# Attention and MoE on one core: softmax weights of the first four pairs turned on TensorE instead of VectorE, products with v over 128 keys, order refitted

## The chip, the cores and the metric

One NeuronCore of a Trainium2 chip runs the whole program in one launch. The metric is the device time of that launch in microseconds; lower is better. Engines are named as in the profile: PE (matmul), PEld (its weight loads), DVE, ACT, POOL, and SP, which issues the DMAs.

## The reference

Inputs are q, k, v of 4 batches x 8 heads x 576 positions x 64, and two MoE matrices, 512 x 2048 and 2048 x 512, all float32.

```python
q_rot, k_rot = rotate(q), rotate(k)              # rotary embedding over the 64 head dims
scores = q_rot @ k_rot.T / sqrt(64)
attn = exp(scores - max(scores));  attn = attn / (sum(attn) + 1e-9)
x = concat_heads(attn @ v)                       # 2304 tokens x 512
h = x @ w_in                                     # 2304 x 2048
g = h * sigmoid(1.702 * h)
out = g @ w_out                                  # 2304 x 512
```

## The kernel before

The 32 heads are worked in 16 pairs; four pairs make one batch. For a pair, `prep_qk` (L413) loads q and k, rotates them on POOL or DVE (rope, L441 to L445), turns them on PE (L450) and copies them to KP (L349 on ACT, L351 on DVE). `scores` (L480) makes a pair's nine tiles of 128 queries x 576 keys (eight of one head each, the ninth with the last 64 queries of both) on PE (L492) into SPS, a PSUM buffer of two banks. `softened` (L500) takes each tile through three steps: DVE negates it into the SBUF tile TP and keeps the minimum (L505), ACT takes the exponential and its sum in place (L508), DVE turns it in place, block by block of 32 x 32 (L511). `weighted` (L535) then multiplies by v over 32 keys at a time: v is loaded to 32 partitions (L470) and copied from there to the other three groups of 32 (L476, the tile VR), and each of 18 key blocks takes eight small matmuls, four row groups by two column halves (L559). The results go to XS (`bring`, L569). `inverse_sums` (L514) brings the reciprocal sums through DRAM to all partitions (r_dram), and `attention` (L589) multiplies, splits the result into a rounded part and its remainder, and stores both to x_dram (L604).

Beside that, 32 weight blocks are loaded, repaired in their bits and split into two float32r parts (`weight`, L612), the first sixteen of them ahead of the MoE. `moe` (L659) works on 256 tokens: it loads both parts of x (XC, L665) and, for each of 16 blocks of 128 hidden units, does twelve matmuls (L681), tanh on ACT (L687), DVE and POOL steps, and six matmuls with w_out (L698). The last four token blocks go through `two_chunks` (L746), which saves products by sums and differences (L822, L863). The first token block needs all four pairs of the first batch.

No order is written out by hand. A planner (`Plan`, L74) knows each step's durations and buffers, and places on each engine, among the steps that are ready, the one with the lowest priority number; the table of numbers at L19 to L38 sets these. Every engine then runs its list strictly in that order. Buffers have few slots: SPS three, PT (one PSUM bank each) two, TP and XS two for the first four pairs (L40, L41) and one later. `n_wide` = 4 marks the first four pairs: only for them may all slots of SPS and PT be taken, since the MoE does not run yet.

Of the kernel before, what the change touches and what calls it, by code (L numbers as in the profile page):

```python
# [10 lines left out]
F32 = mybir.dt.float32  # L11
F32R = mybir.dt.float32r
# [6 lines left out]
PLANNED = dict(wait=300.0, wait_dve=300.0, wait_pool=300.0, n_split=2, n_early=4, n_warm=12, n_wide=4, n_pv0=4,  # L19
               n_pv=2, rope=67526.1, turn=28154.573, raw=-70793.084, v_at=35677.739, exp=95827.369, across=-2250.108,  # L20
               pv_at=88.518, pv_step0=-3821.97, pv_step=41180.485, out_at=-37554.001, prep_s1=48754.242,
               prep_s2=50905.361, sums=-2.997, x_at=0.024, w_raw=12434.947, tanh=-73344.369, g_hi=-83328.381,
               mm2=13528.64, x_load=-38305.217, sums_at=-58928.512, shared_at=-58312.958, t_load=41561.566)
PREP_AT = [-431652, -283537, -243401, 152515, -30818, 30946, 226554, 310380, 369343, 400429, 415121, 453550, 556628,
           575478, 633426, 708309]
PAIR_AT = [-193357, -46411, 4523, 116548, 19858, -52329, -18421, 357094, 447016, 101083, 572080, -23019, 84854,
           402937, 548884, 761647]
PAIR_LEN = [70053, 59678, 65344, -45458, 29105, 157197, 13871, -7478, -59624, -167984, 31814, 209302, 102692, 16421,
            10423, 16592]
MOE_AT = [76876, 312003, 14034, -137881, 278470, 398587, 756302, -263235, 109992, 344381, 521867]  # L30
MOE_STEP = [-765, -55664, -95070, 45956, -63589, 17457, 21326, 60007, 15778, -45369, -18925]
WEIGHT_AT = [-287246, -91871, -93899, -9546, 127995, -371991, -66861, 623510, -246095, 46024, -89938, -116240, 184586,
             513457, -13419, 329611, -149145, 169832, -968684, 64148, 311802, 196893, 295771, 136903, 179235, -30254,
             106295, 327664, 338864, 49395, 458477, 614589]
WEIGHT_FROM = [-100755, 45903, 44044, 8010, 38392, 72497, 110866, 45430, -16026, -66328, -27523, 52698, -161139,
               -28138, -71686, -137246, 51453, 98771, -24675, 29431, 84389, 66452, -49724, 101137, -31460, -18730,
               -83530, 2900, -63136, 114168, -16225, 45606]
T_AT = [292094, -401508, 518576, 614296, 354139, 589559, 140258, 949997]  # L38
MORE_TIMES = ['T_AT']
SLOTS = dict(SPS=3, PT=2, RAW=2, RAW1=1, BT=1, KP=2, ST=2, RT=3, XS=1, XC=4, T=1, G=1, O=2, OW=2, CW=2, TP=1, VR=1)  # L40
EARLY = dict(RAW=2, RAW1=1, BT=1, XS=1, KP=1, TP=1, VR=1, OW=3, CW=3)  # L41
# [32 lines left out]
class Plan:  # L74
# [24 lines left out]
    def op(self, durs, fn, deps=(), bufs=(), prio=0.0, moved=None, chain=None, columns=0.0,  # L99
           release=0.0, port=(), mode=("", ""), code=0.0):  # L100
        o = Op(len(self.ops), durs, fn, list(bufs), prio, moved, columns, release, port, mode, code)
        for d in {id(d): d for d in deps if d is not None}.values():
            d.out.append(o)
            o.before += 1
        if chain is not None:
            if chain in self.chains:
                self.chains[chain].then.append(o)
                o.before += 1
            self.chains[chain] = o
        for b in o.bufs:  # L110
            b.users.append(o)
        self.ops.append(o)
        return o
# [172 lines left out]
def attention_moe(ctx: ExitStack, tc: tile.TileContext, q, k, v, w_in, w_out, cos_sin, out):  # L286
# [17 lines left out]
                 XS=([128, 2, S], F32), XC=([128, KD, CT], F32R), TP=([128, 9, S], F32), VR=([128, 2, S // 32, D], F32),  # L304
# [101 lines left out]
    constants = op(POOL, 1200.0, f, prio=-1e6)  # L406

# [53 lines left out]
    def prep(n):  # L461
        p0 = PREP_AT[n]
        is_early = n < at["n_early"]
        kq_of[n], st_of[n], vr = buf("KP", is_early), buf("ST", is_early), buf("VR", is_early)
        kq_ready[n] = [prep_qk(n, s, p0 + (0.0, at["prep_s1"], at["prep_s2"])[s]) for s in range(3)]
        b, j = divmod(n, PPB)

        def f():
# [31 lines left out]
    def softened(n, t, s, mm, prio):  # L500
# [9 lines left out]
            bufs=[st, tp], prio=prio + at["exp"], extra=228)  # L510
        return o, vec("DVE", "psum", S, lambda e: nc.vector.transpose(tp.t[:, t], tp.t[:, t]), o, bufs=[tp],  # L511
# [23 lines left out]
    def weighted(n, turned, xs, prio):  # L535
# [5 lines left out]
        if n < at["n_wide"]:  # L541
            held = plan.buf("SPS"), plan.buf("PT"), plan.buf("PT")
            banks = lambda: (held[0].t[:, 0], held[0].t[:, 1], held[1].t, held[2].t)
        else:
            held = plan.buf("SPS", (0, 1)), plan.buf("SPS", (0, 1))
            banks = lambda: tuple(x.t[:, i] for x in held for i in range(2))
        n_key, o = S // 32, None
        n_part, step = (at["n_pv0"], at["pv_step0"]) if n < at["n_wide"] else (at["n_pv"], at["pv_step"])
        runs = lambda h, i: (0, 4 + (i < 2)) if not h else (4 + (i < 2), 9)
        for part in range(n_part):  # L550
            keys = range(n_key * part // n_part, n_key * (part + 1) // n_part)

            def f(keys=keys):
                for a in keys:
# [7 lines left out]
            o = pe(f, turned, vr_ready[n], o, f32=[160] * len(keys), each_code=11 if n < at["n_early"] else 8, extra=90.0,  # L562
                   mode=("small", "small"),
# [3 lines left out]
        last = lambda i: slice(512 + 32 * (i % 2), 544 + 32 * (i % 2))  # L567
# [4 lines left out]
        for m in range(2):  # L572
            r, c0, c1 = slice(64 * m, 64 * m + 64), 32 * m, 128 * (1 - m)
            src = held[m]
            if n < at["n_wide"] and m:
                for i in range(2):
                    x = held[1 + i]
                    bring(x, 128, lambda x=x: x.t[:, c0:c0 + 128].rearrange("p (t q) -> p t q", t=4), lambda i=i: tiles()[:, 2 + i])
                    bring(x, 32, lambda x=x: x.t[r, c1:c1 + 32], lambda i=i: xs.t[r, 1, last(i)])
                continue  # L580
# [4 lines left out]
        return done  # L585

    x_written = {}

    def attention(n):  # L589
# [4 lines left out]
        done = weighted(n, [x[2] for x in got], xs, p0 + at["pv_at"] * u)  # L594
# [377 lines left out]
```

## Time and profile before

| | |
|---|---|
| median of 3 runs | 696.7 us (696.59 to 701.07) |
| the profiled execution's own time | 697.98 us |
| its span, first to last instruction | 696.3 us |
| mean granted PE clock | 0.962 |
| busy: PE / DVE / ACT / POOL | 645.9 / 488.3 / 350.3 / 265.5 us |

The profile is of one execution. Busy times are the union of an engine's instructions, so that overlapping ones count once; the means of a group count each in full. A matmul in float32 leaves two records of matmul and two of weight loads in the trace. The granted clock is the share of full speed that PE was given, 0.5 or 1.0 at any moment (1.2 or 2.4 GHz).

### The profile page before, as it was taken

The page shows a single profiled execution, that of the slowest core. Times are in us where ns is not written, and L with a number is a line of the kernel's source. Part 1 is how long each engine was busy: PE and PEld are TensorE (multiplying, and loading weights), DVE is VectorE, ACT ScalarE, POOL GpSimd, SP SyncE. Part 2 cuts the span into 40 slices and gives each one's busy share as a digit, 9 for nine tenths or more (in the row PEclk, how much of TensorE's full clock was granted, in tenths as well). Part 3 has the DMA queues.
Part 4 walks back from the last instruction along what each step waited for, and adds up shares of the span by engine and source line. Part 5 has one row for each costly group of instructions (what it writes and reads, how often), then busy time and mean ns, then how long its engine had stood idle before and what let it go on. Part 6 is the DMA issues. An engine that isn't in the chain of part 4 may idle for free.

```text
span 696.3 us, 19494 instructions
## 1 busy us (share of the span) xinstructions
PE 645.9 (93%) x7928; PEld 524.7 (75%) x7928; DVE 488.3 (70%) x1070; ACT 350.3 (50%) x863; POOL 265.5 (38%) x269
## 2 busy tenths in 40 slices
PE   6588776899999999999999999999999999999996
PEld 4356553777778777788887878787878899988985
DVE  4998998698899888968966583847369544644342
ACT  2776766375576554545445352544234444543343
POOL 3776675364745354667644531220102100120000
PEclk8888987799999999999999999999999999999999
DMA  7866786956866655394556450543076223342111
GB/s 150 212 191 162 185 207 199 242 155 155 256 173 187 149 168 157 127 339 144 150 188 163 119 120 20 124 123 79 11 274 213 74 109 122 121 169 75 61 62 60
DMA packets 98506, 104.35 MB, mean 150 GB/s; under 512 B 62560, under 2 KB 82288, under 8 KB 93808
## 3 DMA queue, kind: packets, MB, share of 16 engines
q1 hardware_dynamic: 98416, 103.10, 51.7%
q8 instruction: 62, 1.02, 0.6%
q14 instruction: 28, 0.23, 0.1%
HBM read 65.26 MB, written 23.67 MB: 128 GB/s over the span
## 4 chain that ended last, share of the span: by engine, by line
PE 73%; DVE 8%; DMA 5%; issue 4%; POOL 3%; SPq 3%; ACT 3%; DVEq 0%; POOLq 0%; ACTq 0%
PE PT L681 15%; PE SPS L698 13%; PE SPS L863 13%; PE SPS L559 10%; PE SPS L492 9%; PE SPS L822 6%; PE PT L822 5%; DVE TP L505 2%; DVE TP L511 2%; PE PT L450 2%; DMA t_dram<-TS 1%; SPq L531 1%; DMA OW<-in_moe_w_out_dram 1%; DMA XS<-r_dram 1%; POOL RAW L354 1%
## 5 line engine op out<-in xcount | busy, mean ns | idle before, releaser
L681 PEld LDWEIGHTS PT<-XC,win 128*128 128x128 f32 x960 | 125.7, 193 | 21.2 <-issue 10.9
L681 PE MATMUL PT<-XC,win 128*128 128x256 f32 x960 | 136.3, 291 | 3.6 <-issue 2.6
L698 PE MATMUL SPS<-wout,G 128*128 128x512 f32 x480 | 132.6, 406 | 2.8 <-DVE G L354 1.4
L508 ACT ACTIVATE TP<-TP,ST 128x576 f32<-128x576 f32 x144 | 110.8, 771 | 46.3 <-DVE TP L505 46.0
L492 PE MATMUL SPS<-KP 64*128 64x288 f32 (+1 forms) x640 | 111.2, 457 | 10.9 <-DVE TP L505 9.1
L511 DVE STREAM_TRANSPOSE TP<-TP 128x576 f32<-128x576 f32 x144 | 108.3, 768 | 15.9 <-ACT TP L508 15.7
L505 DVE TENSOR_SCALAR_CACHE_REDUCE TP<-SPS 128x576 f32<-128x576 f32 x144 | 103.5, 747 | 10.6 <-PE SPS L492 10.0
L698 PEld LDWEIGHTS SPS<-wout,G 128*128 128x128 f32 x480 | 83.7, 189 | 29.8 <-issue 8.7
L559 PE MATMUL SPS<-TP,VR 32*64 32x128 f32 (+1 forms) x4032 | 96.3, 304 | 4.5 <-issue 2.9
L559 PEld LDWEIGHTS SPS<-TP,VR 32*64 32x64 f32 x4032 | 84.3, 136 | 15.6 <-issue 10.2
L863 PE MATMUL SPS<-wout,G 128*128 128x512 f32 x384 | 93.0, 392 | 0.0
L492 PEld LDWEIGHTS SPS<-KP 64*128 64x128 f32 (+1 forms) x640 | 58.1, 188 | 45.2 <-DVE TP L505 17.7
L354 DVE TENSOR_TENSOR G<-T,G 128x256 fp32r<-128x256 f32 x122 | 57.4, 483 | 43.1 <-ACT G L342 32.6
L863 PEld LDWEIGHTS SPS<-wout,G 128*128 128x128 f32 x384 | 70.4, 188 | 13.9
L342 ACT CAST G<-T 128x256 fp32r<-128x256 f32 x115 | 44.9, 404 | 57.2 <-PE SPS L698 38.3
L648 POOL TENSOR_TENSOR CW<-CW 128x512 int32<-128x512 int32 x32 | 41.4, 1300 | 58.4 <-DVE RAW L354 17.9
L354 POOL TENSOR_TENSOR XS<-XS 128x576 fp32r<-128x576 f32 (+1 forms) x25 | 35.6, 1423 | 61.0 <-DVE XS L344 39.5
L687 ACT ACTIVATE T<-PT 128x256 f32<-128x256 f32 x80 | 30.4, 380 | 53.5 <-PE PT L681 39.6
L689 DVE SCALAR_TENSOR_TENSOR T<-T,PT 128x256 f32<-128x256 f32 x80 | 32.7, 409 | 33.3 <-ACT T L687 33.1
L354 POOL TENSOR_TENSOR U<-U,U 128x256 f32<-128x256 f32 x15 | 11.6, 772 | 113.3 <-ACT U L342 111.4
L354 POOL TENSOR_TENSOR BT<-RAW,cos_sin_sb 128x512 f32<-128x512 f32 (+1 forms) x30 | 31.9, 1063 | 29.5 <-DMA RAW<-in_k_dram 9.8
L450 PE MATMUL PT<-ident,RAW 128*128 128x128 f32 x144 | 26.3, 298 | 17.4 <-issue 6.8
(94 smaller groups left out, 853.9 us busy)
## 6 DMA issues: line engine op xcount, KB each, us to landing
TR<-t_dram SPq DMA_DIRECT2D x16, 1024.0 KB, 4.8
VR<-VR SPq DMA_DIRECT2D x48, 288.0 KB, 4.0
x_dram<-XS SPq DMA_DIRECT2D x16, 576.0 KB, 4.6
XC<-x_dram SPq DMA_DIRECT2D x18, 512.0 KB, 5.3
OW<-in_moe_w_in_dram SPq DMA_DIRECT2D x16, 512.0 KB, 5.0
OW<-in_moe_w_out_dram SPq DMA_DIRECT2D x16, 512.0 KB, 5.2
t_dram<-TS SPq DMA_DIRECT2D x8, 1024.0 KB, 5.9
VR<-in_v_dram SPq DMA_DIRECT2D x32, 144.0 KB, 3.5
```

What stands on the lines that cost most here:

```text
L342: return nc.scalar.copy(to, src)
L354: return engine[e].tensor_tensor(to, a, b, op=how)
L492: nc.tensor.matmul(ss[h].t[:, c, 0:HALF] if t < 4 else ss[h].t[rows, c, 0:HALF], kq.t[rows, 1, t * 128:t * 128 + (128 if t < 4 else 64)], ...
L505: o = vec("DVE", "psum", S, lambda e: nc.vector.tensor_scalar(tp.t[:, t].rearrange("p (c s) -> p c s", c=2), s.t[:, :, 0:HALF], -1.0, LARG ...
L508: o = vec("ACT", "sbuf", S, lambda e: nc.scalar.activation(tp.t[:, t], tp.t[:, t], AF.Exp, bias=st.t[:, 0, t:t + 1], scale=-1.0, accum_out ...
L511: return o, vec("DVE", "psum", S, lambda e: nc.vector.transpose(tp.t[:, t], tp.t[:, t]), o, bufs=[tp], prio=prio + at["exp"] + at["across"])
L559: nc.tensor.matmul(bank[64 * h:64 * h + 64, to:to + 32 * (s1 - s0)], vr.t[rows, h, a], tp.t[rows, s0:s1, 32 * a:32 * a + 32], start=(a == ...
L648: o = vec("POOL", "two", DM, lambda e, a=a, r=r: nc.gpsimd.tensor_tensor(a().bitcast(I32), a().bitcast(I32), r(), op=ALU.add), o, low, buf ...
L681: nc.tensor.matmul(h.t[:, 0:CT], win[f_i // KH][:, wl, kk, f_i % KH * 128:(f_i % KH + 1) * 128], xc[xl].t[:, kk, :], start=(i == m == 0), ...
L698: nc.tensor.matmul(acc.t[:, m, :], g.t[:, a, m * 128:(m + 1) * 128], wout[f_i // KH][:, b, f_i % KH, :], start=(f_i == fs[0] and i == 0), ...
L822: nc.tensor.matmul(h(to), w(a)[:, k], x(b)[:, k], start=(begin and n == 0), stop=(n == 5), skip_group_check=True)
L863: nc.tensor.matmul(acc[j].t[:, m, :], g.t[:, x, m * 128:(m + 1) * 128], wout[f_i // KH][:, y, f_i % KH, :], start=(begin and n == 0), stop ...
```

## The change

For the first four pairs the DVE turn of L511 is gone. In the new `weighted_whole` PE turns each tile's first 512 keys in four 128 x 128 blocks into PT, and ACT or DVE copies them back to the same place of TP; the last 64 keys of eight tiles are turned in pairs, and the ninth tile's by two more. v is loaded once with keys on 128 partitions (the tile VE, two slots; the last 64 keys of both heads share one block, with zeros beside them from POOL), and the products run over 128 keys, one column half of the array for each head. They use one SPS buffer and no PT. KP gets one slot more for the first pairs, and all numbers of the planner's table are new, with a list of single adjustments (NUDGE) beside them.

```diff
-PLANNED = dict(wait=300.0, wait_dve=300.0, wait_pool=300.0, n_split=2, n_early=4, n_warm=12, n_wide=4, n_pv0=4,
+PLANNED = dict(wait=300.0, wait_dve=300.0, wait_pool=300.0, n_split=2, n_early=4, n_warm=12, n_wide=4, n_pv=2,
...
+NUDGE = {240: -4973, 292: -1266, 328: 1607, 399: -5780, 422: -10019, 423: 6925, 1070: 1165, 1071: 9102, 1139: 3669,
...
-EARLY = dict(RAW=2, RAW1=1, BT=1, XS=1, KP=1, TP=1, VR=1, OW=3, CW=3)
+EARLY = dict(RAW=2, RAW1=1, BT=1, XS=1, KP=2, TP=1, VE=2, OW=3, CW=3)
...
+        prio = prio + NUDGE.get(len(self.ops), 0.0)
...
+        for x in plan.tiles["VE"]:
+            nc.gpsimd.memset(x[0:64, 4, 1], 0.0)
+            nc.gpsimd.memset(x[64:128, 4, 0], 0.0)
...
+            for h in range(2):
+                nc.sync.dma_start(vr.t[:, 0:4, h], v[b, 2 * j + h, 0:512].rearrange("(t p) d -> p t d", p=128))
+                nc.sync.dma_start(vr.t[64 * h:64 * h + 64, 4, h], v[b, 2 * j + h, 512:576])
...
+        if n < at["n_wide"]:
+            return o, o
         return o, vec("DVE", "psum", S, lambda e: nc.vector.transpose(tp.t[:, t], tp.t[:, t]), o, bufs=[tp],
...
-        if n < at["n_wide"]:
-            held = plan.buf("SPS"), plan.buf("PT"), plan.buf("PT")
-            banks = lambda: (held[0].t[:, 0], held[0].t[:, 1], held[1].t, held[2].t)
...
+    def weighted_whole(n, ready, xs, prio, turn_at):
...
+        def turn(cols, get, ready, moves, pr):
+            pt = plan.buf("PT")
+
+            def f():
+                for i in range(cols // 128):
+                    src = get(i)
+                    for h, x in enumerate(src):
+                        r = both(h) if len(src) > 1 else slice(0, 128)
+                        nc.tensor.matmul(pt.t[r, 128 * i:128 * i + 128], x, ident, start=(i == 0), stop=(i == cols // 128 - 1),
+                                         is_transpose=len(src) == 1, skip_group_check=True)
...
+            for width, to, src in moves:
+                turned.append(vec("ACT DVE", "psum", width, lambda e, to=to, src=src: copy(e, to(), src(pt.t)), o,
+                                  bufs=[tp, pt], prio=pr + at["across"]))
...
+        for t, o in ready.items():
+            turn(512, lambda i, t=t: [tp.t[:, t, 128 * i:128 * i + 128]], o,
+                 [(512, lambda t=t: tp.t[:, t, 0:512], lambda x: x)], turn_at[t])
...
+        av, o = plan.buf("SPS"), None
+        for part in range(2):
+            def f(part=part):
+                for kt in (0, 1) if part == 0 else (2, 3):
+                    for h in range(2):
+                        nc.tensor.matmul(av.t[both(h), 0, :], ve.t[:, kt, h], tp.t[:, 5 * h:5 * h + 4, 128 * kt:128 * kt + 128],
+                                         start=(kt == 0), stop=False, skip_group_check=True)
...
+        return [vec("ACT DVE", "psum", w, lambda e, c=c, w=w: copy(e, xs.t[:, 1, 512 * c:512 * c + w], av.t[:, c, 0:w]), o,
+                    bufs=[av, xs], prio=pr) for c, w in ((0, 512), (1, 64))]
```

Line numbers of the new kernel are higher: the eviction L505 is L527, the exponential L508 is L530, ACT's and DVE's copies L342 and L344 are L346 and L348, the scores L492 are L514, the sums' turn L524 is L548, the turn of q and k L450 is L462. New are the turn L615 and the products L639 (512 columns), L643, L649 and L652.

On DVE, in the first pair (TP_101), evictions and turns stood in turn before the change:

```order
L505 TENSOR_SCALAR TP_101,ST_95<-SPS_65 128x576
L505 TENSOR_SCALAR TP_101,ST_95<-SPS_67 128x576
L351 TENSOR_SCALAR KP_94<-PT_68 128x512
L511 STREAM_TRANSPOSE TP_101<-TP_101 128x576
L505 TENSOR_SCALAR TP_101,ST_95<-SPS_65 128x576
L505 TENSOR_SCALAR TP_101,ST_95<-SPS_66 128x576
L511 STREAM_TRANSPOSE TP_101<-TP_101 128x576
```

And now, at the same tiles:

```order
L527 TENSOR_SCALAR TP_101,ST_95<-SPS_65 128x576
L527 TENSOR_SCALAR TP_101,ST_95<-SPS_66 128x576
L348 COPY TP_101<-PT_68 128x512
L527 TENSOR_SCALAR TP_101,ST_95<-SPS_65 128x576
L527 TENSOR_SCALAR TP_101,ST_95<-SPS_67 128x576
L527 TENSOR_SCALAR TP_101,ST_95<-SPS_66 128x576
L348 COPY TP_101<-PT_68 128x512
```

The turns are gone from DVE; of the 36 wide copies back eight stand on it, and 28 on ACT.

On PE, between the second pair's scores (KP_94) and the first pair's products, the order before was:

```order
L492 MATMUL SPS_65<-KP_94 128x288
L492 MATMUL SPS_66<-KP_94 128x288
L450 MATMUL PT_68<-ident,RAW_107 128x128 x4
L524 MATMUL PT_69<-ident,ST_95 9x128
L559 MATMUL SPS_67<-TP_101,VR_102 64x160 x2
L559 MATMUL PT_68<-TP_101,VR_102 64x128
L559 MATMUL PT_69<-TP_101,VR_102 64x128
```

And now:

```order
L514 MATMUL SPS_65<-KP_94 128x288
L514 MATMUL SPS_67<-KP_94 128x288
L615 MATMUL PT_68<-ident,TP_113 128x128 x4
L548 MATMUL PT_69<-ident,ST_95 9x128
L639 MATMUL SPS_66<-TP_101,VE_114 64x512 x2
L643 MATMUL SPS_66<-TP_101,VE_114 64x64 x2
L639 MATMUL SPS_66<-TP_101,VE_114 64x512 x2
L643 MATMUL SPS_66<-TP_101,VE_114 64x64 x2
L615 MATMUL PT_68<-ident,TP_113 128x128 x4
L615 MATMUL PT_69<-ident,TP_113 128x128 x4
```

Where 144 small matmuls of a pair stood there are 20 large ones, and between them, and between the score groups, stand turns of the next pair's tiles, which take both PT slots.

On SP, at the first loads of XC, the order before was (the store of the fourth pair's result to x_dram stands six rows ahead of this piece):

```order
L431 DMA RAW_91<-in_k_dram 64x64
L665 DMA XC_70<-x_dram 128x4x256
L665 DMA XC_71<-x_dram 128x4x256
L526 DMA r_dram<-RT_97 9x128
L665 DMA XC_72<-x_dram 128x4x256
```

And now (XS_110 holds the fourth pair's result):

```order
L681 DMA x_dram<-XS_110 128x2x576
L439 DMA RAW_90<-in_q_dram 128x4x64 x2
L709 DMA OW_117<-in_moe_w_in_dram 128x4x256
L550 DMA r_dram<-RT_97 9x128
L742 DMA XC_70<-x_dram 128x4x256
L742 DMA XC_71<-x_dram 128x4x256
```

The fifth pair's reciprocal sums (r_dram) now go out ahead of the first XC loads and not behind two of them. Before the first MoE matmul PE has the same sets of work in both kernels, the scores and products of five pairs, and one score group of the sixth more in the new one.

## Rows read from the trace of the kernel before

**Rows 1.** The page: busy time, and busy tenths and granted clock in 40 slices
```profile
PE 645.9 (93%) x7928; PEld 524.7 (75%) x7928; DVE 488.3 (70%) x1070; ACT 350.3 (50%) x863; POOL 265.5 (38%) x269
...
PE   6588776899999999999999999999999999999996
...
DVE  4998998698899888968966583847369544644342
...
PEclk8888987799999999999999999999999999999999
```

**Rows 2.** Busy us by stage: length, engines (instructions), granted clock, DMA share, GB/s
```profile
0.00:128.30 128.30, 94.25 (x1733) 66.06 (x1733) 110.84 (x242) 77.35 (x185) 74.56 (x74) 0.84 0.74 188
128.30:139.00 10.70, 8.05 (x39) 6.35 (x40) 5.11 (x11) 4.93 (x12) 4.63 (x5) 0.68 1.00 254
139.00:348.00 209.00, 202.91 (x2772) 161.47 (x2770) 181.09 (x378) 120.88 (x284) 118.72 (x114) 0.99 0.64 180
348.00:696.30 348.30, 340.67 (x3394) 290.87 (x3390) 191.28 (x441) 147.13 (x382) 67.56 (x79) 1.00 0.36 114
```

**Rows 3.** Chain of waits, end of the first stage: start us, us, what
```profile
117.07 1.35 DVE TP L511 x2
...
120.67 4.40 PE SPS L559 x119
...
125.66 2.65 PE SPS L559 x111
128.31 0.55 PE PT L681 x3
128.87 2.65 issue
131.51 2.29 PE PT L681 x9
```

**Rows 4.** Groups by line, shapes apart, 0 to 128.3 us: busy us, mean ns, idle before
```profile
L511 DVE STREAM_TRANSPOSE TP<-TP 128x576 f32<-128x576 f32 x45 | 33.6, 766 | 4.1 <-ACT TP L508 4.0
L505 DVE TENSOR_SCALAR_CACHE_REDUCE TP<-SPS 128x576 f32<-128x576 f32 x45 | 32.2, 745 | 3.4 <-PE SPS L492 3.3
L349 ACT ACTIVATE KP<-PT 128x512 f32<-128x512 f32 x11 | 6.5, 596 | 16.4 <-PE PT L450 16.3
L351 DVE TENSOR_SCALAR KP<-PT 128x512 f32<-128x512 f32 x3 | 2.0, 674 | 0.0
L342 ACT COPY XS<-SPS 128x256 f32<-128x256 f32 x4 | 1.4, 355 | 0.0
L344 DVE COPY XS<-PT 128x128 f32<-128x128 f32 x4 | 1.0, 261 | 0.0
L342 ACT COPY XS<-SPS 64x64 f32<-64x64 f32 x4 | 0.8, 204 | 0.0
```

**Rows 5.** PE in order of time, scores (L492) and turns (L450): start us, us
```profile
51.53 0.66 PE L450 MATMUL PT<-ident,RAW 128*128 128x128 f32 x4
52.12 0.75 PE L492 MATMUL SPS<-KP 64*128 64x288 f32 x2
...
66.84 2.36 PE L492 MATMUL SPS<-KP 64*128 64x288 f32 x16
```

**Rows 6.** Busy us in three short stretches of the first stage, columns as in rows 2
```profile
0.00:10.00 10.00, 5.53 (x29) 4.94 (x29) 4.28 (x8) 2.22 (x4) 1.60 (x8) 1.00 0.66 139
60.00:65.00 5.00, 5.00 (x92) 3.95 (x98) 4.74 (x12) 3.38 (x8) 3.02 (x4) 0.50 0.64 220
95.00:100.00 5.00, 5.00 (x70) 3.29 (x75) 4.57 (x9) 3.44 (x10) 4.54 (x4) 0.50 0.92 183
```

**Rows 7.** DMA issues, 0 to 128.3 us: count, KB each, us to landing
```profile
VR<-VR SPq DMA_DIRECT2D x15, 288.0 KB, 4.0
```

**Rows 8.** SP's queue in order of time: start us, us, what it issued
```profile
115.38 0.37 SPq L604 DMA_DIRECT2D x_dram<-XS  x1
...
121.91 2.05 SPq L665 DMA_DIRECT2D XC<-x_dram  x2
```

More of the change, by code (lines that the diff above doesn't have):

```diff
@@ L24 @@
[L24 to L37, printed above, removed]
@@ L560, in f @@
                                              tp.t[rows, s0:s1, 32 * a:32 * a + 32], start=(a == 0), stop=(a == n_key - 1))
-            o = pe(f, turned, vr_ready[n], o, f32=[160] * len(keys), each_code=11 if n < at["n_early"] else 8, extra=90.0,
-                   mode=("small", "small"),
+            o = pe(f, turned, vr_ready[n], o, f32=[160] * len(keys), each_code=8, extra=90.0, mode=("small", "small"),
                    bufs=[*held, tp, vr], prio=prio + part * step)
@@ L566, in weighted @@
         tiles = lambda: xs.t[:, 1, 0:512].rearrange("p (t i q) -> p i t q", t=4, i=4)
-        last = lambda i: slice(512 + 32 * (i % 2), 544 + 32 * (i % 2))
         def bring(src, width, get, to):
             done.append(vec("ACT DVE", "psum", width, lambda e: copy(e, to(), get()), o, bufs=[src, xs], prio=pr))
-        for m in range(2):
+        for m, src in enumerate(held):
             r, c0, c1 = slice(64 * m, 64 * m + 64), 32 * m, 128 * (1 - m)
[L574 to L580, printed above, removed]
             bring(src, 256, lambda src=src, c0=c0: src.t[:, :, c0:c0 + 128].rearrange("p i (t q) -> p i t q", t=4),
@@ L585, in weighted, with f @@
         return done
+    def weighted_whole(n, ready, xs, prio, turn_at):
+        tp, ve = tp_of[n], vr_of[n]
+        turned = []
+        both = lambda h: slice(64 * h, 64 * h + 64)
+        def turn(cols, get, ready, moves, pr):
+            pt = plan.buf("PT")
+            def f():
+                for i in range(cols // 128):
[4 more added lines that the diff above has]
+                                         is_transpose=len(src) == 1, skip_group_check=True)
+            n_t, halves = cols // 128, len(moves) > 1
+            o = pe(f, ready, constants, tr=[128] * n_t * (not halves), f32=[128] * n_t * halves, beside=halves,
+                   each_code=1 + halves, mode=("half", "half") if halves else ("", ""), bufs=[tp, pt], prio=pr + at["across"])
+            for width, to, src in moves:
[4 more added lines that the diff above has]
+                 [(512, lambda t=t: tp.t[:, t, 0:512], lambda x: x)], turn_at[t])
+        wide = lambda x: x.rearrange("p (t a q) -> p t a q", t=4, a=2)
+        turn(512, lambda i: [tp.t[:, i + 5 * h, 512:576] for h in range(2)], [ready[t] for t in ready if t != 4],
+             [(256, lambda a=a: tp.t[:, 5 * a:5 * a + 4, 512:576], lambda x, a=a: wide(x)[:, :, a]) for a in range(2)],
+             turn_at[3])
+        turn(128, lambda i: [tp.t[:, 4, 512:576]] * 2, ready[4],
+             [(64, lambda h=h: tp.t[both(h), 4, 512:576], lambda x, h=h: x[both(h), both(h)]) for h in range(2)], turn_at[4])
+        av, o = plan.buf("SPS"), None
[5 more added lines that the diff above has]
+                                         start=(kt == 0), stop=False, skip_group_check=True)
+                    for h in range(2):
+                        c0 = 128 * kt + 64 * h
+                        nc.tensor.matmul(av.t[both(h), 1, 0:64], ve.t[:, kt, h], tp.t[:, 4, c0:c0 + 64], start=(kt == 0),
+                                         stop=False, skip_group_check=True)
+                if part == 0:
+                    return
+                out = av.t[:, 0].rearrange("p (t a q) -> p t a q", t=4, a=2)
+                for a in range(2):
+                    nc.tensor.matmul(out[:, :, a], ve.t[:, 4].rearrange("p h d -> p (h d)"), tp.t[:, 5 * a:5 * a + 4, 512:576],
+                                     start=False, stop=(a == 1), skip_group_check=True)
+                for h in range(2):
+                    nc.tensor.matmul(av.t[both(h), 1, 0:64], ve.t[both(h), 4, h], tp.t[both(h), 4, 512:576], start=False,
+                                     stop=True, skip_group_check=True)
+            o = pe(f, turned, vr_ready[n], o, f32=[512, 64] * 2 + ([256, 256, 64] if part else []), beside=4, each_code=2,
+                   extra=200.0 * part, mode=("half", "half"), bufs=[av, tp, ve], prio=prio + part * at["pv_step0"])
+        pr = prio + 2 * at["pv_step0"] + at["out_at"]
+        return [vec("ACT DVE", "psum", w, lambda e, c=c, w=w: copy(e, xs.t[:, 1, 512 * c:512 * c + w], av.t[:, c, 0:w]), o,
+                    bufs=[av, xs], prio=pr) for c, w in ((0, 512), (1, 64))]
```

49 lines of the change are left out of this document (37 added, 12 removed).

## The prediction

> **What bounds the kernel now.** I read the page first, then the busy time by stage, then the chain of waits at the end of the first stage, then the groups by line inside it. On the page the reader sees PE busy 93% of the span and the others far less [rows 1]; the slices show where that mean is wrong: DVE is at 9 tenths nearly from the start, PE is not until about the eighth slice, and only ahead of that is its granted clock below full for long. The stage table says it in numbers [rows 2]. Before the first MoE product (0 to 128.3 us) DVE is busy 110.8 of 128.3 us, PE 94.3 at a mean granted clock of 0.84, ACT 77.4, POOL 74.6. After 139 us PE is busy 202.9 of 209.0 and 340.7 of 348.3 us at the full clock. So there are two kernels in one. The late one is bound by PE, and its 80 and 64 hidden blocks, twelve of the sixteen pairs' turns and all MoE products are the same before and after the change. The early one is bound by DVE, and what it saves moves everything behind it forward. It really ends at 131.5 us: the chain [rows 3] goes through DVE's 32x32 transposes at 117.07, the products of the fifth pair (120.67 to 128.31), three MoE matmuls, and 2.65 us in which PE waits for nothing that the profile names.
>
> **The change, part by part.** Durations are means of the groups of the first stage [rows 4]. An engine's instructions overlap a little, so that the means add up to more than its busy time (on DVE some 123 us against 110.8, on ACT some 90 against 77.4); I scale by 0.90 and 0.86.
>
> DVE loses 36 transposes (9 tiles of each of four pairs), 36 x 0.766 = 27.6 us, and six small copies out of PT, 4 x 0.261 and 2 x about 0.2 = 1.4 us. It gets 8 of the 36 wide copies back from PSUM at 0.674 (the copy of 512 columns to KP), 5.4 us, four of 256 columns, which lie between 0.261 for 128 and 0.674 for 512, say 0.40, 1.6 us, and two of 64 at about 0.2. Net -21.6, scaled -19.4: 110.8 becomes 91.4. The new order puts two evictions of the sixth pair ahead of the first MoE product (2 x 0.745) and a few rope steps more on DVE: about 93.
>
> ACT gets 28 wide copies at 0.596, 16.7 us, four of 256 columns at 0.355, and six of 64 at about 0.2, 19.3 in all; its copies of the results shrink from eighteen small ones (ten at 0.2, four at 0.26, four at 0.355, 4.5 us) to four of 512 and four of 64 columns (3.2). Net +18.0, scaled +15.5: 77.4 becomes 93.
>
> So DVE and ACT come out equal, at 93 us. Were everything else free, the stage would be as long as DVE's 93 and the 17.5 us that DVE idles in it today: 17.5 us less. That is the good end.
>
> PE is the price. At the full clock two score groups of 8 records follow each other in 2.36 us [rows 5], 1.18 us each for 2 x 288 columns in two row groups, 2.05 ns a column; four turns of 128x128 take 0.59 us (51.53 to the next start at 52.12). Half a pair's old products take 2.65 us [rows 3], a pair 5.3. The new products stream, with the two column halves side by side, 4 x (512 + 64) + 2 x 256 + 64 = 2880 columns; at the 1.84 ns of the old products (2.65 us for 9 keys of 160 columns) that is 5.3 us: nothing gained or lost. On top come 36 turns, 9 x 0.59 = 5.3 us, and ten matmuls for the last 64 columns, two at a time, 5 x 128 columns, 1.2 us. That is +6.5 us a pair, +26 us for four. No row shows a transposed weight block read back from PSUM in place, so its bounds are taken from these rows: if PE keeps today's mixed clock, its work is 94.3 + 26 = 120 us, and with the 4.5 us that it idles in the first 10 us [rows 6] and the 3.2 us after 128.3 the stage does not get shorter than 128: 3.5 us gained at most, and nothing if it has to wait once more. If it runs at the full clock throughout, 94.3 x 0.84 = 79, +26 = 105, and with the same 7.7 us the stage ends at 113: 18.5 gained. I take the middle between the two ends and a little of the doubt, -8.5: the stretches at half clock (60 to 65 and 95 to 100 us, busy all of 5 us at 0.50 [rows 6]) come behind gaps in which PE waited for an eviction, and the turns now lie in such gaps; but they also wait for exponentials and copies, which are on an ACT that has little slack left.
>
> The new waits: a turn on PE waits for the tile's exponential on ACT, and behind it in PE's order stand the turns of q and k and the next scores, for which DVE waits; the products wait for the last copies, thirteen a pair. A copy on ACT waits for PE, and behind it stand exponentials and the weights' conversion. PT has two slots and is now taken eleven times more a pair, about 0.6 us for the turns and 0.6 for the copy each: 44 x 1.2 = 53 us of 2 x 120, no bound by itself.
>
> DMA: the replication of v goes for four pairs, 12 of the 15 transfers of 288 KB in the stage [rows 7], and with it five issues a pair become four. Nothing in the chain at the end of the stage waits for them, so I count 0; they give SP and the queues room. The four memsets on POOL lie at the start, where it waits for data: 0. More slots for KP and v: 0, or a little inside the middle value.
>
> Behind the stage the refitted order does the same PE work; PE idles 13.7 us of 557 there [rows 2]. A new fit can win or lose 3; I take -0.5.
>
> Sum: -8.5 - 0.5 = -9.0 against the profiled execution's own 697.98 us (span 696.3), 689.0; that execution lies 1.3 us above the median of 696.7, so 688 in the measure of the runs.
>
> **Where a rule speaks against it.** The old products put eight tiles on the array, four row groups by two column halves. Were the halves serial, 9 keys would be 9 x 288 columns in 2.65 us [rows 3], 1.02 ns a column, half of what the score rows [rows 5] show; so the halves do run side by side there. The Trainium skill (TensorE: Matmul & The Clock Gate, Part 3, "What overlaps and what doesn't") says that a weight load overlaps matmuls in flight only when its row group differs. The new halves share all four row groups, which no row of this trace shows; by that rule they could go one after the other, and the time would be that of the third rival.
>
> **The rivals.**
> 1. All engines pack as well as DVE does today. For it: DVE is busy 90% of the stage now. Against: three engines at once would have to be above 85%. Stage -13 to -18: 679 to 684.
> 2. The gain is hidden. PE stays at half clock after its waits, or the first MoE product waits for its data: the store of the fourth pair's result is issued at 115.38, the loads of XC at 121.91, and PE goes on at 131.51 [rows 3, 8], 16 us behind the store; in the new SP order the store and the fifth pair's r_dram stand right ahead of those loads, and PE has only two score groups left behind that pair's products. Then -4 to +2: 693 to 699.
> 3. Slower: the column halves run one after the other. Each pair then streams 4 x 2 x (512 + 64) + 2 x 256 + 2 x 64 = 5248 columns, 9.7 us for 5.3, +17.6 us for four. PE's bounds become 105 + 17.6 + 7.7 = 130 and 120 + 17.6 + 7.7 = 145 against 131.5: about +7, 704. It decides from the point where PE's 26 us grow beyond some 37 (131.5 - 7.7 less the 94.3 or 79 us of today's work leaves 30 to 45). For it: the new tiles share their rows. Against: the old ones' halves overlap.
> 4. The change does what it says, but the new order in the late stage loses more than 3 us of PE time: 692 to 700. Against: the kinds and counts of its PE work are the same.
>
> **How the numbers follow.** The forecast (684 to 692) has 0.50, the first rival 0.12, the second 0.24, the third 0.08, the fourth 0.06. Faster or slower by over 1% (7.0 us, about what a measurement of this kernel can tell from no change) means below 689.7 or above 703.7. Below lie the first rival and three quarters of the forecast, 0.12 + 0.38, and 0.03 of the rest: 0.53. Above lie half of the third rival and a little of the fourth: 0.06. Between: 0.41. The range from 680 to 698 leaves out some 0.04 below and 0.13 above.
>
> **What would show it.** Right: the first MoE product moves from 128.3 to about 119 and PE goes on at about 122.5; up to there DVE and ACT are both busy for 90 to 95 us, PE for 100 to 112 at a granted clock above 0.88; the new products of a pair take 5 to 6 us at the full clock, four turns 0.6. Wrong: products of 9 us or more (rival 3); PE busy but at a clock of 0.84 or less, or a gap of over 4 us before the first MoE products that ends with XC (rival 2); a late stage (first MoE product to end) that differs from today's 565 us by more than 3 us (rival 4).

## The result: 691.0 us, 1.2% faster

The changed kernel takes 690.99 us (median of 10 runs, 687.18 to 696.65), the kernel before 699.24 beside it (10 runs, 696.59 to 702.1): ratio 0.9885, 95% interval [0.9852, 0.9918]. The forecast was 688.0 for 696.7, a ratio of 0.9875. The profiled execution of after takes 691.52 us (span 689.8, 6.5 less than before's 696.3).

The page of after: busy time, and tenths and granted clock in 40 slices, against [rows 1].

```profile
PE 658.0 (95%) x7160; PEld 527.4 (76%) x7160; DVE 472.6 (69%) x1032; ACT 361.9 (52%) x891; POOL 267.8 (39%) x283
...
PE   6999986999979999989999999999999999999997
...
PEclk8899998899999999999999999999999999999999
```

PE is at 9 tenths from the second to the fifth slice, where it was at 5 to 8, and its clock at 0.9 from the third to the sixth, where it was mostly 0.8. PE does 12.1 us more work (645.9 to 658.0) in a span 6.5 us shorter: it idles 18.6 us less (50.4 to 31.8).

Busy us by stage in after, columns as in [rows 2]; the first row ends with the first MoE product.

```profile
0.00:122.30 122.30, 106.40 (x973) 68.51 (x973) 101.20 (x223) 91.59 (x215) 69.58 (x72) 0.93 0.66 178
122.30:132.00 9.70, 9.70 (x47) 7.30 (x46) 6.79 (x17) 5.05 (x13) 5.82 (x7) 0.77 0.77 174
132.00:348.00 216.00, 205.94 (x2827) 162.74 (x2829) 186.69 (x381) 123.69 (x295) 127.56 (x130) 0.98 0.64 185
348.00:689.80 341.80, 335.91 (x3332) 288.88 (x3316) 177.93 (x414) 141.54 (x370) 64.83 (x77) 1.00 0.35 109
```

Up to the first MoE product PE idles 15.9 us (122.30 - 106.40) instead of 34.05 (128.30 - 94.25). From 122.3 to 132.0 PE has no gap (9.70 of 9.70 us), where in before it stood still again until 131.51 [rows 3].

The chain of waits of after at the end of the first stage (start, us, what), against [rows 3]:

```profile
108.66 0.70 DVE TP L535
...
109.40 4.40 PE SPS L579 x120
...
117.85 2.21 issue
120.06 2.29 PE SPS L514 x7
122.35 2.86 PE PT L758 x12
```

The fifth pair's products start at 109.40 instead of 120.67. A score group of the sixth pair now stands between them and the MoE, which comes without the 2.65 us gap behind its first matmuls; a gap of 2.21 us lies inside that score group, behind its first record.

Groups of after by line, 0 to 122.3 us, against [rows 4]:

```profile
L358 DVE TENSOR_TENSOR BT<-RAW,cos_sin_sb 128x512 f32<-128x512 f32 x10 | 6.9, 687 | 6.0 <-DMA RAW<-in_q_dram 3.9 <-POOL RAW L358 1.2 <-DMA RAW<-in_k_dram 1.0
L535 DVE STREAM_TRANSPOSE TP<-TP 128x576 f32<-128x576 f32 x9 | 6.4, 747 | 0.3 <-ACT TP L530 0.3
L348 DVE COPY TP<-PT 128x512 f32<-128x512 f32 x8 | 5.4, 687 | 0.3 <-PE PT L615 0.2
L358 DVE TENSOR_TENSOR RAW<-RAW,BT 128x512 f32<-128x512 f32 x6 | 5.1, 858 | 1.3 <-POOL RAW L358 1.2
...
L358 DVE TENSOR_TENSOR XS<-XS 128x576 f32<-128x576 f32 x2 | 2.6, 1303 | 0.2 <-ACT XS L346 0.2
...
L358 DVE TENSOR_TENSOR XS<-XS 128x576 fp32r<-128x576 f32 x1 | 1.9, 1855 | 0.0
...
L346 ACT COPY TP<-PT 128x512 f32<-128x512 f32 x28 | 15.8, 594 | 0.5 <-ACT TP L530 0.4
```

The copies cost what was forecast (687 and 594 ns for 674 and 596). What is new on DVE is L358 (L354 in before), operations with two sources: some take longer than in before (858 ns for 684, 1303 for 758, 1855 for 757).

PE of after in order of time, one pair's products (start, us), against [rows 5]:

```profile
79.19 1.08 PE L639 MATMUL SPS<-TP,VE 128*64 128x512 f32 x4
...
80.21 1.03 PE L639 MATMUL SPS<-TP,VE 128*64 128x512 f32 x4
...
81.78 0.60 PE L615 MATMUL PT<-ident,TP 128*128 128x128 f32 x4
...
85.47 0.33 PE L652 MATMUL SPS<-TP,VE 64*64 64x64 f32 x4
85.73 0.44 PE L615 MATMUL PT<-ident,TP 128*64 128x128 f32 x4
```

From 79.19 to 85.73, less the 1.03 us of other work from 81.28 to 82.31, a pair's products take 5.5 us.

### The profile page after: what moved, and what is told of

Read it like the earlier page. It is cut to its first block, busy times and chain, and to the rows that moved or that the text cites. A ratio compares the mean times of both kernels' runs of the same rounds, so it can differ in the third digit from the quotient of the medians.

```text
span 689.8 us, 18009 instructions
## 1 busy us (share of the span) xinstructions
PE 658.0 (95%) x7160; PEld 527.4 (76%) x7160; DVE 472.6 (69%) x1032; ACT 361.9 (52%) x891; POOL 267.8 (39%) x283
## 4 chain that ended last, share of the span: by engine, by line
PE 80%; DVE 5%; ACT 4%; DMA 4%; issue 2%; SPq 2%; POOL 2%; DVEq 0%; ACTq 0%; POOLq 0%
PE PT L758 15%; PE SPS L775 14%; PE SPS L940 13%; PE SPS L514 10%; PE SPS L579 9%; PE SPS L899 6%; PE PT L899 6%; DMA OW<-in_moe_w_out_dram 2%; PE PT L615 2%; PE PT L462 2%; PE SPS L639 2%; ACT TP L530 1%; DVE TP L527 1%; DVE TP L535 1%; DMA t_dram<-TS 1%
## 5 line engine op out<-in xcount | busy, mean ns | idle before, releaser
L530 ACT ACTIVATE TP<-TP,ST 128x576 f32<-128x576 f32 x144 | 111.4, 776 | 43.5 <-DVE TP L527 43.4
L527 DVE TENSOR_SCALAR_CACHE_REDUCE TP<-SPS 128x576 f32<-128x576 f32 x144 | 103.7, 748 | 15.5 <-PE SPS L514 15.2
L514 PE MATMUL SPS<-KP 64*128 64x288 f32 (+1 forms) x640 | 105.8, 445 | 5.8 <-DVE TP L527 2.7
L535 DVE STREAM_TRANSPOSE TP<-TP 128x576 f32<-128x576 f32 x108 | 81.7, 768 | 10.7 <-ACT TP L530 10.2
L358 DVE TENSOR_TENSOR G<-T,G 128x256 fp32r<-128x256 f32 x118 | 54.3, 474 | 41.8 <-ACT G L346 38.5
L514 PEld LDWEIGHTS SPS<-KP 64*128 64x128 f32 (+1 forms) x640 | 55.4, 184 | 36.0 <-DVE TP L527 8.6
L346 ACT CAST G<-T 128x256 fp32r<-128x256 f32 x115 | 44.8, 404 | 59.6 <-PE SPS L775 44.2
L579 PE MATMUL SPS<-TP,VR 32*64 32x160 f32 (+1 forms) x3456 | 68.2, 298 | 2.8 <-issue 2.4
L358 POOL TENSOR_TENSOR U<-U,U 128x256 f32<-128x256 f32 x16 | 12.1, 758 | 144.5 <-ACT U L346 118.6
L579 PEld LDWEIGHTS SPS<-TP,VR 32*64 32x64 f32 x3456 | 60.6, 133 | 9.3 <-issue 6.5
L358 POOL TENSOR_TENSOR XS<-XS 128x576 fp32r<-128x576 f32 (+1 forms) x27 | 38.4, 1423 | 70.7 <-DVE XS L348 26.5
L764 ACT ACTIVATE T<-PT 128x256 f32<-128x256 f32 x80 | 30.5, 381 | 53.2 <-PE PT L758 41.4
L358 POOL TENSOR_TENSOR RAW<-RAW,cos_sin_sb 128x512 f32<-128x512 f32 (+1 forms) x32 | 31.6, 988 | 21.2 <-DMA RAW<-in_k_dram 5.5
L929 ACT ACTIVATE T<-U 128x256 f32<-128x256 f32 x64 | 26.0, 418 | 20.9 <-DVE U L358 15.1
```

The source lines that it names most:

```text
L346: return nc.scalar.copy(to, src)
L358: return engine[e].tensor_tensor(to, a, b, op=how)
L514: nc.tensor.matmul(ss[h].t[:, c, 0:HALF] if t < 4 else ss[h].t[rows, c, 0:HALF], kq.t[rows, 1, t * 128:t * 128 + (128 if t < 4 else 64)], ...
L527: o = vec("DVE", "psum", S, lambda e: nc.vector.tensor_scalar(tp.t[:, t].rearrange("p (c s) -> p c s", c=2), s.t[:, :, 0:HALF], -1.0, LARG ...
L530: o = vec("ACT", "sbuf", S, lambda e: nc.scalar.activation(tp.t[:, t], tp.t[:, t], AF.Exp, bias=st.t[:, 0, t:t + 1], scale=-1.0, accum_out ...
L579: nc.tensor.matmul(bank[64 * h:64 * h + 64, to:to + 32 * (s1 - s0)], vr.t[rows, h, a], tp.t[rows, s0:s1, 32 * a:32 * a + 32], start=(a == ...
```

## The experiments

First MoE product and the rest of the span (us) are from the profiled execution, ratio and interval from all runs; each kernel's ratio is to runs of before taken beside it.

| kernel | first MoE product | rest | median | ratio to before |
|---|---|---|---|---|
| before | 128.2 | 568.1 | 699.24 | 1 |
| after | 122.3 | 567.5 | 690.99 | 0.9885 [0.9852, 0.9918] |
| e1 new code, old numbers | 130.3 | 608.3 | 742.37 | 1.0643 [1.0602, 1.0684] |
| e2 old code, new numbers | 149.1 | 576.7 | 725.82 | 1.0397 [1.0348, 1.0447] |
| e6 before, short turns | 127.9 | 564.5 | 696.74 | 0.9988 [0.9963, 1.0013] |
| e10 before, no copies of v | 128.4 | 567.4 | 694.09 | 0.9958 [0.9933, 0.9982] |
| e11 before, both | 128.6 | 564.4 | 694.43 | 0.9956 [0.993, 0.9982] |
| e3 after, halves apart | 130.1 | 566.0 | 697.84 | 1.0008 [0.9971, 1.0045] |
| e4 after, short copies | 123.2 | 568.2 | 692.98 | 0.9912 [0.9881, 0.9942] |
| e5 after, one block turned | 126.2 | 566.4 | 692.31 | 0.9921 [0.9891, 0.9951] |
| e12 after, both | 123.6 | 563.3 | 689.24 | 0.9899 [0.9867, 0.9931] |
| e7 after, traffic put back | 127.6 | 567.6 | 693.1 | 0.9936 [0.9912, 0.9961] |
| e8 after, one load early | 122.3 | 564.6 | 687.95 | 0.9825 [0.977, 0.988] |
| e9 after, four loads early | 122.5 | 569.2 | 689.48 | 0.9908 [0.9876, 0.9941] |

The first stage repeats well: e8 and e9 don't touch it, and it ends at 122.3 and 122.5, as in after (122.3). But one thing hides in the column. PE's gap that the profile calls "issue" lies ahead of the first MoE product in after and its variants, and behind it in before and its variants, and its length differs: 2.21 us in after, 3.66 in e3, 2.42 in e4, 4.57 in e5, 3.11 in e12, 2.10 in e7. Without it the stages of after, e4, e5, e12, e7 and e3 would end at 120.1, 120.8, 121.6, 120.5, 125.5 and 126.4.

**The two halves of the change (e1, e2).** The new code with the old table and no NUDGE, and the old code with the new table.

> New structure with the planner's numbers of the kernel before and no single adjustments. If the structure makes the gain (turns off DVE), the first MoE product still comes 5 to 10 us earlier than 128.3 and the time is 689 to 695 us against about 698 of before. If the refit makes it, the old numbers give no gain or a loss, 697 to 710 us.

> Structure of the kernel before with the new table of numbers (without the single adjustments, which belong to the new steps). If the structure makes the gain, this is not faster than before: 697 to 715 us, first MoE product at 128 us or later. If the numbers make it, 688 to 693 us.

Each alone is far slower. The first MoE product in e1, with new code and the old order (form of the row: count, ns, first and last start):

```profile
L756 PE MATMUL PT<-XC,win x240: 274/282/580, 130.3 to 238.1; 128*128 128x256 f32 x120
```

So the new code under the old numbers does not shorten the first stage at all (130.3 for 128.2), and loses 40 us behind it; the new numbers lengthen the old code's first stage by 21. The 6 us exist only in both together. NUDGE is in neither half, and two things were not run: the new code and table without NUDGE, and a new search of numbers for the old code. So how much a better order alone could give the old code is open.

**Is DVE the bound of before (e6)?**

```diff
-tp.t[:, t], tp.t[:, t]
+tp.t[:, t, 0:64 if n < 4 else S], tp.t[:, t, 0:64 if n < 4 else S]
```

> The kernel before, with DVE's turns of the first four pairs cut from 576 to 64 columns (that part of the turn is left out); order unchanged. It takes some 20 us off DVE and adds nothing elsewhere. If DVE bounds the first stage, the stage ends 10 to 17 us earlier: 681 to 690 us. If the stage is a chain of waits in which DVE is only busy, 4 us at most: 693 to 699 us.

Busy us of e6 up to its first MoE product, columns as in [rows 2]:

```profile
0.00:127.90 127.90, 94.32 (x1733) 66.30 (x1733) 96.92 (x242) 76.75 (x185) 74.59 (x74) 0.84 0.73 187
```

DVE's waits in e6 from 10 to 128 us (total, times, longest):

```profile
DVE TP L511 <- ACT TP L508: 12.9, 21, 2.7
DVE TP L505 <- PE SPS L492: 5.2, 6, 1.3
```

13.9 us of DVE's work are gone (110.84 to 96.92), and the stage ends 0.3 us earlier. The time turned into waits: DVE now waits 12.9 us for exponentials, where [rows 4] has 4.0. DVE was 86% busy and yet, under this order, not what set the end.

**The copies of v, and both (e10, e11).** Under the old order again; e11 also has the diff of e6.

```diff
+LEFT_OUT = (1, 2, 3)
...
+        nc.gpsimd.memset(plan.tiles["VR"][1], 0.0)
...
+                if n not in LEFT_OUT:
                     nc.sync.dma_start(vr.t[32 * i:32 * i + 32], vr.t[0:32])
```

> The kernel before, where the second, third and fourth pair leave out the replication of v (9 of the 15 transfers of 288 KB of the first stage; their products read the slot as it stands, so their results are not computed); order, transposes and products as before. POOL clears one v slot at the start, beside its wait for data. If the replication held the first stage (its transfers and its issues stand ahead of the experts' weights in SP's queue), the first MoE product comes at 123 to 125 us instead of 128.2, and the time falls by 3 to 5 us. If DVE's work sets the stage, as predicted, it stays at 127 to 129 and the time within 1.5 us. If only both together hold it, no change here and a gain in the next run.

> The kernel before with both edits: no replication of v for the second to fourth pair and the DVE transposes of the first four pairs cut to 64 columns (both parts left out of the computation). If DVE and the transfers hold the stage in turn, each hiding the other, the first MoE product comes at 115 to 121 us, further than in either kernel with one edit. If the transfers alone hold it, it comes where the kernel without copies has it, within 1.5 us. If neither does, and the order between DVE's maximum, ACT's exponential and the next pair's scores does, it stays above 126.

Busy us of e11 up to its first MoE product:

```profile
0.00:128.60 128.60, 95.43 (x1733) 66.16 (x1733) 95.62 (x242) 76.93 (x185) 76.82 (x75) 0.84 0.63 167
```

With 15 us of DVE's work and nine transfers less, the stage ends at the same time. The medians of both gain some 3 us; the stage does not show it (and e10's profiled execution, 697.55 us, is the slowest of its ten), so its place is open. Why nothing moves is seen on the engines that were not touched. One instruction of POOL in before (in brackets the idle time ahead and what ended it):

```profile
109.25 1.27 POOL L648 TENSOR_TENSOR CW<-CW 128x512 int32<-128x512 int32 x1 [7.46 <-DVE RAW L354]
```

The same one in e11:

```profile
109.61 1.26 POOL L651 TENSOR_TENSOR CW<-CW 128x512 int32<-128x512 int32 x1 [7.80 <-DVE RAW L355]
```

The 68 arithmetic instructions of POOL up to 128 us start within -0.4 and +0.6 us of before's in e6, e10 and e11. SP's queue, two loads of the experts' weights in before (start, us):

```profile
57.55 1.62 SPq L632 DMA_DIRECT2D OW<-in_moe_w_out_dram  x2
...
102.53 0.36 SPq L632 DMA_DIRECT2D OW<-in_moe_w_out_dram  x1
```

The same two in e11:

```profile
57.35 1.56 SPq L635 DMA_DIRECT2D OW<-in_moe_w_out_dram  x2
...
102.24 0.37 SPq L635 DMA_DIRECT2D OW<-in_moe_w_out_dram  x1
```

SP got ahead and then waited for DVE's repair of an earlier block, which frees one of the three slots (the rows' columns: total, times, longest; 10 to 122 us). In before, and then in e11:

```profile
SPq L632 <- DVE CW L645: 4.2, 4, 1.3
...
SPq L635 <- DVE CW L648: 11.5, 5, 5.9
```

ACT of before stands behind the last of these loads; the next exponential stands behind eight more instructions in its list, at 111.69:

```profile
106.93 0.69 ACT L636 ACTIVATE CW<-OW 128x512 int32<-128x512 uint32 x1 [6.10 <-DMA OW<-in_moe_w_out_dram]
```

POOL waits for DVE, because the kernel orders POOL's two-source operations behind DVE's by hand. Every engine runs its list in order, and so one relieved engine arrives early at the next such wait. That these loops set the stage's length fits all rows here, but is argued: shorter POOL instructions, or another number of weight slots, were not tried.

**Column halves apart (e3).** In each part all matmuls of one head, then all of the other.

```diff
-                for kt in (0, 1) if part == 0 else (2, 3):
-                    for h in range(2):
+                for h in range(2):
+                    for kt in (0, 1) if part == 0 else (2, 3):
```

> In each half of a pair's products all matmuls of one column half now come before those of the other; same matmuls, same order otherwise. If the two column halves run side by side in the changed kernel, a pair's products go from about 5.3 to 9 us or more, PE gets some 15 us more in the first stage, of which PE's idle time there covers a part: 697 to 707 us. If shared row groups had kept them one after the other anyway, no change: 689 to 693 us.

Group of the 512-column products in e3, up to its first MoE product (busy us, mean ns):

```profile
L639 PE MATMUL SPS<-TP,VE 128*64 128x512 f32 x64 | 23.6, 606 | 0.0
```

The same group of after:

```profile
L639 PE MATMUL SPS<-TP,VE 128*64 128x512 f32 x64 | 16.3, 604 | 0.0
```

The same 64 records of 605 ns cover 7.3 us more. In after the halves overlap throughout. In e3 the last matmul of one half and the first of the other still do (four records in 1.08 us at 84.13), and the matmul ahead of them stands alone (two records in 1.07 us at 83.10). The stage ends 7.8 us later, 1.5 of it by the longer gap, and the whole gain is lost. With no overlap left the price would be about twice the 7.3 us (an estimate from these rows: four steps of some 1.05 us in each half of a pair's products, for three in e3 and two in after).

**Relief of PE, of ACT and DVE, of all (e5, e4, e12).** One block of four turned, 64 columns copied of 512, and both.

```diff
-                for i in range(cols // 128):
+                for i in range(1 if cols == 512 and len(moves) == 1 else cols // 128):
...
-[(512, lambda t=t: tp.t[:, t, 0:512], lambda x: x)]
+[(512, lambda t=t: tp.t[:, t, 0:64], lambda x: x[:, 0:64])]
```

> The changed kernel, with the 36 wide copies back from PSUM cut from 512 to 64 columns (that part of the copy is left out); order unchanged. It takes some 11 us off ACT and 4 us off DVE. If PE bounds the new first stage, 0 to 4 us come of it: 687 to 692 us. If ACT bounds it, 8 to 13 us: 678 to 684 us.

> The changed kernel, with only the first of the four 128x128 blocks of each wide turn done on PE (three are left out); order unchanged. It takes some 16 us off PE at the full clock. If PE bounds the new first stage, 5 to 12 us come of it: 679 to 686 us. If DVE and ACT do, 3 us at most: 688 to 692 us.

> The kernel after with one block of four turned on PE and the 36 wide copies cut to 64 columns (both parts left out of the computation): PE, ACT and DVE relieved at once. If the three engines were packed against each other, so that relieving one only hands the stage to another, the first MoE product comes at 112 to 118 us instead of 122.3 (123.2 and 126.2 with one edit alone). If the arrival of the experts' weights and the order of the chain from 88 us on hold the stage, it stays at 121 to 126 and the time within 2 us of the two runs with one edit.

e12 up to its first MoE product:

```profile
0.00:123.60 123.60, 96.47 (x865) 58.06 (x865) 98.61 (x222) 82.58 (x215) 68.95 (x70) 0.92 0.65 177
```

PE works 9.9 us less than in after, ACT 9.0, DVE 2.6, and the stage ends 1.3 us later (0.4 without the gap); with one edit alone it ends 0.9 (e4) and 3.9 us later (e5; 0.7 and 1.5 without the gap). That the three engines are packed against each other is refuted as well, under this order. That the order and its loads set the stage instead is argued. In e12's chain of waits loads of the weights stand where after's has PE and ACT, among them this one (start, us):

```profile
49.34 4.06 DMA OW<-in_moe_w_in_dram
```

Most of e5's delay is the gap of 4.57 us inside the fifth pair's products, whose row stands in the last section. The three medians lie within 2 us of after's; e12's is some 3 us below those of e4 and e5, where at most 2 were expected, and its stage doesn't show why.

**Transfers put back (e7).** Three transfers of 256 KB a pair, ahead of the store of the sums.

```diff
+            if n < at["n_wide"]:
+                for i in range(3):
+                    nc.sync.dma_start(spare[n, i], vr_of[n].t[:, 0:4].rearrange("p t h d -> p (t h d)"))
             nc.sync.dma_start(r_dram[n], rt.t)
```

> The changed kernel, with three more transfers of 256 KB a pair for the first four pairs (v's tile to a spare place in DRAM, issued with the pair's reciprocal sums): about the traffic that the single load of v saved. If that traffic was hidden, 0 to 2 us more: 690 to 693 us. If its absence is part of the gain, 4 to 10 us more: 695 to 701 us.

e7's chain of waits:

```profile
42.05 7.30 DMA OW<-in_moe_w_out_dram
...
52.07 4.21 DMA OW<-in_moe_w_in_dram
```

The loads of the weights come late, and not by traffic alone: the three transfers stand ahead of the store of the sums in SP's queue, the load of these sums behind it is issued at 47.52 instead of 44.17, and the next load of weights at 52.07 instead of 48.89. Counted instruction by instruction, ACT and POOL run 5.3 us behind after's from 63 us on, and this slip stays to the end of the stage (127.6 for 122.3). The median is 2 us above after's, with intervals that touch. So taking traffic away from the old order does not move its stage (e10), and putting it into the new one at this place costs 5 us of stage. How much of that is the traffic and how much the place in the queue was not separated.

**A version that may be better (e8, e9).** One load of w_out in the late stage, or four, issued right behind the last use of their slot.

```diff
+        listed = plan.order()
+        for i in (1305, 1341):
+            o = next(x for x in listed if x.idx == i)
+            at_o, slot = listed.index(o), next(b.slot for b in o.bufs if b.pool == "OW")
+            prev = max(j for j in range(at_o) if any(b.pool == "OW" and b.slot == slot for b in listed[j].bufs))
+            listed.insert(prev + 1, listed.pop(at_o))
```

> The changed kernel, with one weight load of the late stage (w_out, issued at 187.2 us, landed 8.7 us later, ACT and behind it PE waiting) issued right after its buffer is free, ahead of three small broadcasts. If the late stage gives back part of the gain by such waits, 2 to 5 us come of it: 686 to 689 us. If another wait takes its place, 1 us at most: 690 to 692 us.

> The kernel after, complete, with every load of experts' weights that the planner puts after 135 us issued right behind the last use of its slot in SP's queue (four loads move, one of them the load already tried alone, 688.0). If late loads hold PE in more than one place of the late stage (PE idles 16 us there, 10.1 of them from 132 to 348 us), the late stage falls from 567.5 to 561 to 564 us and the time to 684 to 687. If only the one load mattered, 687 to 689. If the loads moved forward delay others, 689 to 693.

PE's largest wait in after from 122 to 350 us is for DVE's step behind a tanh, which ACT did late behind a load that took from 187.22 to 195.92:

```profile
PE PT L758 <- DVE T L766: 3.4, 2, 3.1
```

The same wait in e8:

```profile
PE PT L758 <- DVE T L766: 0.3, 1, 0.3
```

The wait is all but gone: counted by ACT's instructions, 3.4 us come back at this place in e8 (190 to 197 us) and 2.3 in e9, which makes the same move and three more. But another wait grew, in after and then in e8:

```profile
PE SPS L514 <- DVE TP L527: 1.7, 2, 1.3
...
PE SPS L514 <- DVE TP L527: 3.9, 2, 3.3
```

The rest of the span is 2.9 us shorter in e8, and not by less idling: PE idles 16.7 us there for after's 16.0, and works 3.7 us less, at a granted clock of 0.98 for 0.94 from 122.3 to 200. e8's 687.95 is the lowest median here, but of four runs (684.6 to 699.53), and its interval overlaps after's; e9 has no clear gain. So e8 beats before clearly; that it beats after is not shown.

## Why the prediction was right, and where its reason was wrong

**Held.** By the prediction's own points the first stage gave 9.2 us (131.51 to 122.35; forecast 8.5). ACT is busy 91.6 us (93), PE 106.4 (100 to 112) at 0.93 (above 0.88). Products take 5.5 us a pair (5.3), four turns 0.6, copies 0.59 and 0.69. PE's +26 us shows as +12.2 of busy time, in the main because the clock rose from 0.84 to 0.93, part of which the forecast counted on. One of its reasons for it is read wrongly: of the two stretches at half clock only the first comes behind a wait for an eviction (2.27 us, until 59.47), the second behind one for POOL (1.43 us, until 94.45).

**The step that failed** is the first: "The early one is bound by DVE, and what it saves moves everything behind it forward." e6 takes 13.9 us from DVE under the old order and gets 0.3; e11 gets none. In its place the runs show that under the old order DVE's work does not set the end of the stage, nor do the copies of v (e10: 128.4), and that only new code and new order together moved the fifth pair's products up by 11.3 us; either alone gains nothing (e1, e2). Which waits hold the old stage is argued and not shown, and how much of the gain the saving on DVE made possible stays open. That 8.5 came so near 9.2 is therefore luck in part: its two ends were derived from engines' busy times, and e12 shows that these don't set the stage after the change either. The 90% that the first rival gives for DVE is 86% by [rows 2].

**Mis-sized: DVE.** Forecast 93, measured 101.2. The turns went as counted (45 to 9). But 32 instead of 26 wide operations of two sources stand on DVE, and some are stretched; the ten groups of that line add up to 30.5 us instead of 22.0. PE's +26 was a little too much: busy time times granted clock goes from 79 (94.25 x 0.84) to 99 us (106.40 x 0.93), 20 more, with one score group more in it.

**DMA at 0** held for the old order (e10) and not for the new one with the transfers where e7 puts them (5.3 us of stage).

**The late stage** was to give 0.5; by the prediction's cut it took 2.7 more (567.5 from 122.35, 564.8 from 131.51), and from the first MoE product on 0.6 less (567.5 for 568.1). One late load costs 2.3 to 3.4 us there (e8, e9). Yet kernels with the same late order as after range from 563.3 to 568.2 (e3, e4, e5, e7, e12): the term lies inside what one profile can tell.

**The rivals.** Full packing didn't come: PE still idles 15.9 us. The gain wasn't hidden by XC, whose loads are issued at 110.56, 12 us ahead:

```profile
106.95 0.37 SPq L681 DMA_DIRECT2D x_dram<-XS  x1
...
110.56 3.31 SPq L742 DMA_DIRECT2D XC<-x_dram  x4
```

The third rival was real but not taken: e3 shows about half its price (+7.8 us of stage, the time of before), and after's order avoids it. 512-column products of both halves ran side by side though they share all row groups, four records of 605 ns in 1.03 to 1.08 us; what counted was that matmuls of the two halves alternate. The Trainium skill (TensorE: Matmul & The Clock Gate, Part 3, "What overlaps and what doesn't") says that a weight load overlaps matmuls in flight only where the row group differs. The trace doesn't agree: the weight loads of both halves go on until 79.38, while the first matmul runs from 79.19:

```profile
79.18 0.20 PEld L639 LDWEIGHTS SPS<-TP,VE 128*64 128x64 f32 x4 [0.17 <-issue]
```

That sentence is on weight loads; that the halves could go serially by it was the prediction's own reading.

## What to carry to other kernels

Where every engine runs a fixed list, a busy share of 86% doesn't make an engine the bound: cut its work under the same order first, and see whether anything behind it moves. Here code and order gained only together, and either alone was 4 and 6% slower, so try them together, and search the old code's order with the same effort before the gain is put down to the code. Leaving transfers out gained the stage nothing under one order, and putting about as many into another cost it 5 us, by their traffic or by their place in the queue.

## What the runs showed of the hardware

**DVE waits behind POOL.** Rows of two engines fit the longest of the stretched operations. POOL of after from 87 to 92 us:

```profile
87.22 1.27 POOL L725 TENSOR_TENSOR CW<-CW 128x512 int32<-128x512 int32 x1 [6.01 <-ACT XS L346]
...
90.41 1.27 POOL L358 TENSOR_TENSOR wout<-CW,wout 128x512 fp32r<-128x512 f32 x1
```

DVE of after at the same time:

```profile
87.25 1.86 DVE L358 TENSOR_TENSOR XS<-XS 128x576 f32<-128x576 f32 x1 [0.17 <-ACT XS L346]
...
90.44 1.85 DVE L358 TENSOR_TENSOR XS<-XS 128x576 fp32r<-128x576 f32 x1
```

The group of the first of these operations in before, 0 to 128.2 us (the second's mean there is 757 ns):

```profile
L354 DVE TENSOR_TENSOR XS<-XS 128x576 f32<-128x576 f32 x1 | 0.8, 758 | 0.9 <-DMA XS<-r_dram 0.9
```

Twice DVE began 0.03 us behind POOL and ended about 0.6 us after it: 1.86 us for 0.76, with two sources on both engines. The Trainium skill (SBUF — State Buffer, "SBUF: two separate sides") says that the port pair that the two share goes to the one that starts first, for its whole instruction. The trace agrees (1.1 us more, out of POOL's 1.27). The kernel's ordering by hand makes POOL wait for DVE and never DVE for POOL, and so doesn't cover this case.

**Gaps called "issue" on PE go with loads of instructions.** In the gap of before from 128.87 to 131.51 [rows 3] the DMA queues show one packet of instructions (packets, MB, share of the queues' time):

```profile
q8 instruction: 1, 0.02, 2.3%
```

And in after from 117.2 to 119.4, around the start of its gap at 117.85:

```profile
q8 instruction: 1, 0.02, 2.7%
```

In e5 PE stops between two matmuls of one group, from 117.61 to 122.18, and there is one such packet there too:

```profile
122.18 0.83 PE L579 MATMUL SPS<-TP,VR 32*64 32x160 f32 x14 [4.57 <-issue]
```

The gaps (2.65, 2.21 and 4.57 us) all lie in or behind the fifth pair's small matmuls. Every kernel here but e2 has such a gap, of 2.1 to 4.6 us, and in each of the thirteen a packet of instructions lies between 0.4 us ahead of the gap and its end. But packets come without a gap too: in before at 121.9 and 133.4, with PE going on. That the load of instructions makes the gap wasn't tried.
